# Windowed attention ahead of a mixture of experts: score and value products over 128 and 64 rows with zeros beside, and a transposition that moves to TensorE

## The chip, the cores and the metric

The kernel runs on one core of a Trainium2 chip. The metric is the device time of one execution in microseconds (us). A core has five engines with a queue of instructions each: TensorE (PE in the rows; its weight loads are PEld), VectorE (DVE), ScalarE (ACT), GpSimd (POOL) and SyncE (SP), which here only starts DMAs. Engines wait for each other through semaphores.

## The reference

```python
# q, k, v: (8 batches, 8 heads, 576 tokens, 64); window = 32; dilation = 4
rel = pos[:, None] - pos[None, :]
mask_plain = (rel >= 0) & (rel < window)                                   # heads 0 to 3
mask_dil = (rel >= 0) & (rel < window * dilation) & (rel % dilation == 0)   # heads 4 to 7
attn = softmax(where(mask, q @ k.T / sqrt(64), -1e9));  out = attn @ v
x = out.transpose(0, 2, 1, 3).reshape(4608, 512)
logits = x @ w_gate                       # (4608, 8)
expert_idx = argmax(logits); gate_w = softmax(logits)[expert_idx]
for e in range(8):                        # at most 80 tokens, those of largest gate_w
    out[tok] = gate_w[tok] * (relu(x[tok] @ w1[e]) @ w2[e])   # other rows stay zero
```

Everything is float32. Each w1[e] is 512 x 1024, each w2[e] 1024 x 512.

## The kernel before

**Attention.** For the dilated heads the host orders the tokens by their residue modulo 4, so that both kinds of head look at 32 keys back. A block of 32 queries then needs 64 keys: its own block and the one before. Work goes in 36 tiles (t). A tile holds four blocks j of 32 queries of the plain heads (hh = 0) and four of the dilated heads (hh = 1), 32 x 4 = 128 partitions by 8 x 64 scores. `plan` says which blocks; a batch is 4.5 tiles.

The steps of a tile, with engine and line:

- `scores` on TensorE: the additive mask goes into PSUM by four products with an identity (L393), then 32 products of 64 rows of q and k, 32 weight columns and 64 keys each (L400). A float32 product stands in the trace as two matmuls, so 32 read as x64.
- `smax`, `sbias` on DVE: maximum over each 64 keys (L407) and its scaled negative (L411).
- `sexp` on ACT: eight exponentials of 128 x 64, each with its own bias (L417).
- `ptrans` on DVE: a transposition in 32 x 32 squares (L421) gives the probabilities with keys on partitions.
- `pv` on TensorE: 16 products of 32 keys, with block-diagonal values `v4` of four heads side by side, 260 columns (64 values and a one for the sum, times four) (L435).
- `raw` on ACT (L443) copies that out of PSUM, `norm_r` on DVE (L447, L448) takes the reciprocal of the sums, `norm` on POOL (L454) multiplies, in two halves; the last tile's two halves are on DVE. x is stored (xs).
- `xtrans` on TensorE (four 128 x 128 transpositions, L460) and `xcopy` on ACT (L485) give x with features on partitions, for the gate.

**Routing.** Per batch: gate products (L532, L538), a softmax and the chosen expert on DVE (L560 to L592), counts (`KLp` L643; `csp` L686, of the last batch `tail`; `pre` L692), then a merge with the best 80 tokens of the earlier batches (TensorE `msa`, `msb`, `msr`, `msl`; one-hot rows `ol`, `or`; the new list `lstf`, L808). A batch's merge needs the one before it. After merge 7 `irow` (L1033) holds the rows to gather.

**Experts.** Weights arrive as 512 KB chunks `wr`, and each is split into a high part `wh` (ACT, L189) and a low part `wl` (DVE or POOL, L191); expert 0's chunks are split in halves of 128 x 512. Rows are gathered (`xg`, L285), transposed (`tx`, L1055) and multiplied three times per chunk (`hp` L1072, `yps` L1104). The 18 `zero_out` DMAs of 512 KB clear the output.

**Order.** Each engine's queue is fixed when the kernel is built: `drive` takes chains of work (tiles, gates, counts, merges, splits), and each time appends the piece with the smallest sum of its estimated start and a penalty from a table of numbers. DMAs from SP go in the order of the code; `load_q`, `load_k`, `load_v` and `load_mask` are called around the scores.

## Time and profile before

| | |
|---|---|
| median of three runs | 346.96 us (342.06 to 353.88) |
| profiled execution, its own time | 343.53 us |
| its span in the profile | 341.8 us |
| mean granted TensorE clock (of full speed) | 0.969 |
| busy: PE, PEld, DVE, ACT, POOL | 89%, 61%, 66%, 62%, 55% of the span |
| attention from the third tile's scores to the last value product | about 17 to 196 us |
| from there to `irow` | about 196 to 231 us |
| experts | about 231 to 342 us |

The own time is 1.73 us above the span: that lies outside the recorded instructions. Rows of the profile are in us from the start of the span, unless ns is said.

### The profile page before, as it was taken

What the parts mean: (1) busy time and instruction counts of PE and PEld (TensorE: products, weight loads), DVE (VectorE), ACT (ScalarE), POOL (GpSimd) and SP (SyncE); (2) the same over time, 40 slices, a digit from 0 to 9 for tenths busy, and PEclk for the clock granted to TensorE, in tenths of its full rate; (3) what the DMA queues carried; (4) which work ended last, traced back from release to release, by engine and by line L of the source; (5) the groups of instructions that cost most, each with busy time, mean ns of one, the idle gap of its engine ahead of it and who ended that gap; (6) DMA issues with size and microseconds to landing.
All of it is one profiled execution on the core that took longest, in us unless ns stands there. A gap on an engine that the chain in (4) does not pass through costs nothing.

```text
span 341.8 us, 12863 instructions
## 1 busy us (share of the span) xinstructions
PE 304.0 (89%) x5255; PEld 207.6 (61%) x5255; DVE 224.4 (66%) x628; ACT 213.3 (62%) x620; POOL 186.6 (55%) x281
## 2 busy tenths in 40 slices
PE   6398899989699897899899988776999999999993
PEld 6364666756566664666567557665566666656561
DVE  4233264858366585487576988731589999999950
ACT  6437486667485656667659960110798798789560
POOL 9012134462752385338629789004597889755613
PEclk9789899999999999999999999986899999999999
DMA  6989988979979999999987594701546999999101
GB/s 187 247 241 315 282 269 282 293 223 315 279 222 288 320 360 382 347 278 343 348 288 273 174 311 188 238 10 40 155 149 180 372 397 365 393 344 357 43 0 38
DMA packets 38731, 86.62 MB, mean 253 GB/s; under 512 B 4368, under 2 KB 15504, under 8 KB 38672
## 3 DMA queue, kind: packets, MB, share of 16 engines
q1 hardware_dynamic: 37392, 83.17, 74.4%
q0 software_dynamic: 1280, 2.62, 2.4%
q8 instruction: 41, 0.67, 0.8%
q14 instruction: 18, 0.15, 0.1%
HBM read 65.59 MB, written 20.19 MB: 251 GB/s over the span
## 4 chain that ended last, share of the span: by engine, by line
PE 68%; issue 10%; DMA 8%; DVE 8%; ACT 3%; POOL 1%; SPq 1%; POOLq 0%; ACTq 0%; DVEq 0%
PE pv L435 20%; PE sc L400 9%; PE hp L1072 9%; PE yps L1104 8%; PE xt L460 6%; DVE wl L191 4%; PE sc L393 3%; DMA mask<-in_mask 2%; PE warm L328 2%; PE lt L532 2%; PE KLp L643 2%; DMA out<-yo,itok 2%; DMA wr<-in_w 2%; DMA k<-in_k 1%; DMA xg<-xs,irow 1%
## 5 line engine op out<-in xcount | busy, mean ns | idle before, releaser
L191 DVE TENSOR_TENSOR wl<-wr,wh 128x1024 fp32r<-128x1024 f32 (+1 forms) x53 | 84.1, 1640 | 6.7 <-ACT wh L189 5.9
L454 POOL TENSOR_TENSOR x<-xr,rc 128x256 f32<-128x256 f32 x70 | 42.5, 629 | 84.1 <-ACT xr L443 44.8
L435 PE MATMUL pv<-v,pts 128*32 128x260 f32 x1152 | 75.8, 393 | 5.6 <-issue 5.1
L417 ACT ACTIVATE ex<-sc,nb 128x64 f32<-128x64 f32 x288 | 65.0, 340 | 22.0 <-DVE nb L411 21.9
L189 ACT CAST wh<-wr 128x1024 fp32r<-128x1024 f32 (+1 forms) x72 | 65.8, 959 | 8.4 <-DMA wr<-in_w 4.1
L435 PEld LDWEIGHTS pv<-v,pts 128*32 128x32 f32 x1152 | 36.9, 110 | 29.3 <-issue 7.9
L191 POOL TENSOR_TENSOR wl<-wr,wh 128x1024 fp32r<-128x1024 f32 (+1 forms) x19 | 43.9, 2315 | 9.3 <-ACT wh L189 9.1
L400 PE MATMUL sc<-k,q 64*32 64x64 f32 x2304 | 40.3, 220 | 1.3 <-issue 1.2
L400 PEld LDWEIGHTS sc<-k,q 64*32 64x32 f32 x2304 | 38.3, 109 | 4.8 <-issue 1.5
L443 ACT COPY xr<-pv 128x520 f32<-128x520 f32 x35 | 21.2, 607 | 28.3 <-PE pv L435 25.6
L407 DVE TENSOR_REDUCE mx<-sc 128x8 f32<-128x512 f32 x36 | 24.4, 678 | 21.6 <-PE sc L400 21.5
L285 POOL DMA_INDIRECT xg<-xs,irow x16 | 23.9, 1493 | 24.7 <-DVE lstf L1035 16.8
L485 ACT COPY xT<-xt 128x256 f32<-128x256 f32 (+5 forms) x114 | 32.9, 400 | 6.3 <-PE xt L460 6.1
L421 DVE STREAM_TRANSPOSE pts<-ex 128x512 f32<-128x512 f32 x36 | 25.3, 704 | 9.7 <-ACT ex L417 8.7
L328 PE MATMUL warm<-ones 128*128 128x128 bf16 x317 | 26.0, 237 | 2.4 <-DVE ones L320 1.0
L460 PE MATMUL xt<-c_ident,x 128*128 128x128 f32 x144 | 24.3, 286 | 4.3 <-issue 3.5
L1072 PE MATMUL hp<-wh,xh 128*80 128x512 f32 x64 | 26.9, 420 | 0.4 <-ACT xh L1062 0.4
L447 DVE TENSOR_SCALAR rc<-xr 128x8 f32<-128x8 f32 x35 | 6.1, 175 | 32.1 <-ACT xr L443 31.9
L1104 PE MATMUL yps<-wh,hlo 128*80 128x512 f32 x64 | 25.4, 397 | 1.1 <-DVE hlo L1092 1.1
L1072 PE MATMUL hp<-wl,xh 128*80 128x512 f32 x64 | 26.1, 409 | 0.0
L1072 PE MATMUL hp<-wh,xl 128*80 128x512 f32 x64 | 26.1, 408 | 0.0
L460 PEld LDWEIGHTS xt<-c_ident,x 128*128 128x128 f32 x144 | 15.2, 140 | 16.8 <-issue 11.7
(133 smaller groups left out, 491.1 us busy)
## 6 DMA issues: line engine op xcount, KB each, us to landing
wr<-in_w SPq DMA_DIRECT2D x64, 512.0 KB, 8.0
v<-in_v SPq DMA_DIRECT2D x72, 130.0 KB, 5.7
...
```

Of the source, the lines that this page charges most:

```text
L189: nc.scalar.copy(hi[:, s], w[:, s])
L191: eng.tensor_tensor(out=lo[:, s], in0=w[:, s], in1=hi[:, s].bitcast(F32), op=ALU.subtract)
L328: nc.tensor.matmul(out=t[:, 0:P], lhsT=ones, rhs=ones, start=True, stop=True, skip_group_check=True)
L400: nc.tensor.matmul(out=ps[32 * c:32 * c + 32, 4 * hh + j, :], lhsT=q[64 * u:64 * u + 64, hh, g, j, :], rhs=k2[b % 2][64 * u:64 * u + 64, 2 ...
L417: nc.scalar.activation(st[t]["ex"][:, m], st[t]["sc"][:, m], AF.Exp, bias=st[t]["nb"][:, m:m + 1], scale=1.0 / float(D) ** 0.5)
L421: nc.vector.transpose(out=pt.rearrange("p a b c d -> p (a b c d)"), in_=st[t].pop("ex").rearrange("p a c -> p (a c)"))
L435: nc.tensor.matmul(out=ps[32 * j:32 * j + 32, hh, 0:HS].rearrange("p (c d) -> p c d", c=4), lhsT=pt[:, hh, j, half, :], rhs=v4[vt // 2 % N ...
L454: eng.tensor_tensor(out=x[:, h], in0=st[t][of][:, h, :, :, 0:D], in1=st[t]["rc"][:, h].unsqueeze(3).broadcast_to([P, 2, 2, D]), op=ALU.mult)
L460: nc.tensor.transpose(out=st[t]["xt"][:, c, :], in_=x[:, c * P:(c + 1) * P], identity=ident)
L485: copy(out=dst, in_=ps[:, HC * hh:HC * hh + HC, col:col + n])
L1072: nc.tensor.matmul(out=fs[e]["hp"][n][0:C], lhsT=a_[:, c, :], rhs=b_[:, sl], start=(c == 0 and q == 0), stop=(c == NKC - 1 and q == 2))
L1104: nc.tensor.matmul(out=fs[e]["y"][0:C], lhsT=a_[:, f, :], rhs=b_[:, sl], start=(f == 0 and q == 0), stop=(f == NFC - 1 and q == 2))
```

## The change

- Scores: q and k now have feature and head of a pair interleaved on the partitions (2d + u). `k2` has a second column plane: on the rows of head u the keys stand in plane u, and the other plane is zero. One product of 128 rows, 32 weight columns and 128 columns gives both heads: 16 products per tile for 32.
- The mask is held once for each different pattern, 128 x 2 x 64, and read by a repeating view; it is loaded in two DMAs.
- Softmax: DVE subtracts the maximum from PSUM into SBUF (`ssub`, L415), and one exponential of 128 x 512 works in place on ACT (L420).
- The probabilities are transposed by four 128 x 128 transpositions on TensorE into a PSUM tile `pT` (L426), and copied out in three pieces, two on ACT (64 partitions x 256, L432) and one on DVE (64 partitions x 512, L434), into two fixed buffers `pts` whose other places stay zero.
- Values: 24 products per tile of 64 keys of two heads, 130 columns (L454), for 16 of 32 keys and 260 columns. `v4` has zeros beside the values in the same way.
- `norm` is one operation per tile for two. The gate and the counts share one PSUM buffer (`lt`), and the gate of a batch waits for the counts of the one before.
- Keys of a batch come in two DMAs, those of batch 0 in three pieces of two. More buffers are cleared at the start (DVE, POOL, ACT).
- Ten `zero_out` DMAs go beside the tiles, one every third tile; eight follow the last tile.
- The table of numbers of `drive` is another, and so is the order of the last batch's blocks.

```diff
-ZR, ZI, IW, W0, W1, W2, XC, SP0 = 2, 18, 8, 40, 15, 30, 1, 2
+ZR, ZI, IW, W0, W1, W2, XC, SP0 = 2, 6, 8, 40, 15, 30, 1, 2
-l_pe, lat, LA, AGE = -0.011, 0.147, 3, 0.165
+l_pe, lat, LA, AGE = -0.011, 0.147, 5, 0.162
...
-        k2 = [qp.tile([P, NG, KW], F32, name=f"k2_{i}") for i in range(2)]
+        k2 = [qp.tile([P, 2, KW + HB], F32, name=f"k2_{i}") for i in range(2)]
-        v4 = [vp.tile([P, 4, 2, 4, 2, D + 1], F32, name=f"v4_{i}") for i in range(NV)]
+        v4 = [vp.tile([P, 2, 4, 2, 2, D + 1], F32, name=f"v4_{i}") for i in range(NV)]
+        pts = [kp.tile([P, 2, 2, 2, 2, 2, 32], F32, name=f"pts_{i}") for i in range(2)]
...
+        KS = (0, 64, 160, HB)
+        kv = [k[:, :, 0:KW].rearrange("p u (a x) -> p u a x", a=2 * NG) for k in k2]
         nc.vector.memset(zero, 0.0)
-        nc.vector.memset(k2[0][:, :, 0:32], 0.0)
+        for u in range(2):
+            nc.vector.memset(kv[0][:, u, :, 0:KS[1]], 0.0)
+        for i in (1, 2):
+            for u in range(2):
+                (nc.vector, nc.gpsimd)[u].memset(kv[0][:, u, :, KS[i]:KS[i + 1]], 0.0)
...
+        for i in range(2):
+            for u in range(2):
+                nc.scalar.copy(v4[i][:, u].rearrange("p c a g d -> p (c a g) d"), z65)
+        for i in range(2):
+            nc.vector.memset(pts[i], 0.0)
+        for u in range(2):
+            nc.gpsimd.memset(k2[1][:, u, 0:KW], 0.0)
+        for u in range(2):
+            nc.gpsimd.memset(v4[2][:, u], 0.0)
+        def load_k(b, lo=0, hi=HB):
+            for u in range(2):
...
-        def load_k(b, lo=0, hi=S):
-            nc.sync.dma_start(k2[b % 2][:, :, 32 + lo:32 + hi], io["k"][b, :, :, lo:hi])
+                    nc.sync.dma_start(kv[b % 2][u::2, u, :, lo:hi], io["k"][b, u].rearrange("d (a x) -> d a x", a=2 * NG)[:, :, lo:hi])
...
         def scores(t):
 
             q = q2[t // 2 % NQ][:, t % 2]
-            ps = ps2.tile([P, 8, 64], F32, tag="sc", name=f"sc_{t}")
-            for c in range(4):
-                rows = slice(64 * (c // 2), 64 * (c // 2) + 64)
-                nc.tensor.matmul(out=ps[32 * c:32 * c + 32].rearrange("p a k -> p (a k)"), lhsT=identb[rows, 32 * c:32 * c + 32],
-                                 rhs=mask[rows, t % TPP].rearrange("p a k -> p (a k)"), start=True, stop=False, skip_group_check=True)
-            for hh in range(2):
+            ps = ps2.tile([P, NG, 2, 2, 32], F32, tag="sc", name=f"sc_{t}")
+            for j in range(4):
+                nc.tensor.matmul(out=ps[32 * j:32 * j + 32].rearrange("p (h g) u a k -> p h (g u) (a k)", h=2), lhsT=identb[:, 32 * j:32 * j + 32],
+                                 rhs=mask[:, sig[t]].unsqueeze(2).broadcast_to([P, 2, 4, 64]), start=True, stop=False, skip_group_check=True)
+            for a in range(NG):
                 for j in range(4):
-                    b, k = qplan[t][hh][j]
-                    for c in range(4):
-                        u, g = c // 2, c % 2
-                        nc.tensor.matmul(out=ps[32 * c:32 * c + 32, 4 * hh + j, :], lhsT=q[64 * u:64 * u + 64, hh, g, j, :],
-                                         rhs=k2[b % 2][64 * u:64 * u + 64, 2 * hh + g, 32 * k:32 * k + 64],
-                                         start=False, stop=True, skip_group_check=True)
+                    b, k = qplan[t][a // 2][j]
+                    o, w = a * S + 32 * (k // 2), HB if k % 2 or k == 0 else HB - 32
+                    nc.tensor.matmul(out=ps[32 * j:32 * j + 32, a], lhsT=q[:, a // 2, a % 2, j, :],
+                                     rhs=k2[b % 2][:, :, o:o + 2 * w].rearrange("p u (r y) -> p u r y", r=2)[:, :, :, 0:32],
+                                     start=False, stop=True, skip_group_check=True)
             st[t] = {"sc": ps}
...
-            nc.vector.tensor_reduce(out=st[t]["mx"], in_=st[t]["sc"], axis=AX.X, op=ALU.max)
-
-        def sbias(t):
-            st[t]["nb"] = sp.tile([P, 8], F32, tag="nb", name=f"nb_{t}")
-            nc.vector.tensor_scalar(out=st[t]["nb"], in0=st[t]["mx"], scalar1=-1.0 / float(D) ** 0.5, scalar2=None, op0=ALU.mult)
-
-        def sexp(t, hh):
-            if hh == 0:
-                st[t]["ex"] = sp.tile([P, 8, 64], F32, tag="ex", name=f"ex_{t}")
-            for m in range(4 * hh, 4 * hh + 4):
-                nc.scalar.activation(st[t]["ex"][:, m], st[t]["sc"][:, m], AF.Exp, bias=st[t]["nb"][:, m:m + 1], scale=1.0 / float(D) ** 0.5)
+            nc.vector.tensor_reduce(out=st[t]["mx"], in_=st[t]["sc"].rearrange("p a u r k -> p (a u) (r k)"), axis=AX.X, op=ALU.max)
+        def ssub(t):
+            st[t]["ex"] = sp.tile([P, NG, 64, 2], F32, tag="ex", name=f"ex_{t}")
+            nc.vector.tensor_tensor(out=st[t]["ex"].rearrange("p a k u -> p a u k"), in0=st[t].pop("sc").rearrange("p a u r k -> p a u (r k)"),
+                                    in1=st[t].pop("mx").rearrange("p (a u) -> p a u", u=2).unsqueeze(3).broadcast_to([P, NG, 2, 64]), op=ALU.subtract)
+        def sexp(t):
+            e = st[t]["ex"].rearrange("p a k u -> p (a k u)")
+            nc.scalar.activation(e, e, AF.Exp, scale=1.0 / float(D) ** 0.5)
 
         def ptrans(t):
-            pt = sp.tile([P, 2, 4, 2, 32], F32, tag="pts", name=f"pts_{t}")
-            nc.vector.transpose(out=pt.rearrange("p a b c d -> p (a b c d)"), in_=st[t].pop("ex").rearrange("p a c -> p (a c)"))
-            st[t]["pt"] = pt
+            st[t]["pT"] = ps1.tile([P, NG, 2, 2, 32], F32, tag="pT", name=f"pT_{t}")
+            ex = st[t].pop("ex")
+            for a in range(NG):
+                nc.tensor.transpose(out=st[t]["pT"][:, a].rearrange("p i e q -> p (i e q)"), in_=ex[:, a].rearrange("p k u -> p (k u)"), identity=ident)
+        def pcopy(t, half):
+            ps = st[t]["pT"].rearrange("p (h g) i e q -> p h g e i q", h=2)
+            if half == 0:
+                for h in range(2):
+                    nc.scalar.copy(pts[t % 2][0:64, h, :, :, h], ps[0:64, h])
+            else:
+                nc.vector.tensor_copy(out=pts[t % 2][64:P].rearrange("p h g e s i q -> p (h g) (e s) i q")[:, :, 1:3],
+                                      in_=ps[64:P].rearrange("p h g e i q -> p (h g) e i q"))
 
         def pv(t):
 
-            pt = st[t]["pt"]
             ps = ps1.tile([P, 2, 512], F32, tag="pv", name=f"pv_{t}")
-            for hh in range(2):
-                for half in range(2):
-                    for j in range(4):
-                        b, k = qplan[t][hh][j]
-                        prev = (b, k - 1) if 32 * k % (S if hh == 0 else S // DIL) else (b, k)
-                        vt, vi = vpos[hh, (b, k) if half else prev]
-                        assert vt // 2 * 2 - 1 <= t and (t <= vt // 2 * 2 + 2 or vt // 2 + NV >= NT // 2)
-                        nc.tensor.matmul(out=ps[32 * j:32 * j + 32, hh, 0:HS].rearrange("p (c d) -> p c d", c=4), lhsT=pt[:, hh, j, half, :],
-                                         rhs=v4[vt // 2 % NV][:, :, vt % 2, vi, hh, :],
-                                         start=(half == 0), stop=(half == 1), skip_group_check=True)
-            st[t]["pv"] = ps[:, :, 0:HS].rearrange("p a (u g d) -> p a u g d", u=2, g=2)
+            work = [[] for _ in range(4)]
+            for j in range(4):
+                for h in ((0, 1), (1, 0))[j % 2]:
+                    b, k = qplan[t][h][j]
+                    assert k % 2 == (j + h) % 2
+                    cols = [(0, k)] + [(1, k - 1)] * (k % 2 == 0 and 32 * k % (S if h == 0 else S // DIL) > 0)
+                    for g in range(2):
+                        for i, (s, kk) in enumerate(cols):
+                            vt, vi = vpos[h, (b, kk)]
+                            assert vt // 2 * 2 - 1 <= t and (t <= vt // 2 * 2 + 2 or vt // 2 + NV >= NT // 2), (t, vt)
+                            work[j].append((h, g, s, vt // 2 % NV, vt % 2 * 2 + vi, i == 0, i == len(cols) - 1))
+            for n in range(max(len(w) for w in work)):
+                for j in range(4):
+                    for h, g, s, vb, vc, first, last in work[j][n:n + 1]:
+                        nc.tensor.matmul(out=ps[32 * j:32 * j + 32, h, 2 * g * (D + 1):2 * (g + 1) * (D + 1)].rearrange("p (u d) -> p u d", u=2),
+                                         lhsT=pts[t % 2][:, h, g, j % 2, s if h == 0 else 1 - s, j // 2, :], rhs=v4[vb][:, :, vc, h, g, :],
+                                         start=first, stop=last, skip_group_check=True)
+            st[t]["pv"] = ps[:, :, 0:HS].rearrange("p h (a d) -> p h a d", a=4)
...
-            x = st[t]["x"].rearrange("p (a g u) d -> p a u g d", a=2, g=2)
-            for h in range(2):
-                eng.tensor_tensor(out=x[:, h], in0=st[t][of][:, h, :, :, 0:D], in1=st[t]["rc"][:, h].unsqueeze(3).broadcast_to([P, 2, 2, D]), op=ALU.mult)
+            eng.tensor_tensor(out=st[t]["x"].rearrange("p (h a) d -> p h a d", h=2), in0=st[t][of][:, :, :, 0:D],
+                              in1=st[t]["rc"].unsqueeze(3).broadcast_to([P, 2, 4, D]), op=ALU.mult)
...
+            while b and not end and ("pre", b - 1) not in ev:
+                yield None
...
-                kps = ps1.tile([P, 512], F32, tag="ct", name=f"KLp_{b}_{i}")
+                kps = ps1.tile([P, 512], F32, tag="lt", name=f"KLp_{b}_{i}")
...
         load_q(0, slice(0, 1))
-        load_k(0, 0, P)
+        load_k(0, 0, KS[1])
         nc.sync.dma_start(identb, io["identb"])
-        load_mask(0)
+        NM = mask.shape[1]
+        load_mask(0, 2)
         load_q(0, slice(1, 2))
-        load_k(0, P, 2 * P)
-        load_mask(1)
+        load_k(0, KS[1], KS[2])
+        nc.sync.dma_start(ident, io["ident"])
+        load_v(0)
         load_q(1)
-        load_k(0, 2 * P, 3 * P)
-        load_v(0)
-        load_mask(2)
-        load_k(0, 3 * P, S)
-        nc.sync.dma_start(ident, io["ident"])
+        load_mask(2, NM)
+        load_k(0, KS[2], KS[3])
         load_v(1)
-        load_mask(3)
...
+            if ZI <= i < NT and i % 3 == 0:
                 zero_out(zeros.pop(0))
+            if i == NT + 1:
+                while zeros:
+                    zero_out(zeros.pop(0))
```

On TensorE, before, around tile 24 (the numbers behind a name are tile and buffer):

```order
L435 MATMUL pv_21_2712<-v4_1_147,pts_21_2621 32x260 x16
L460 MATMUL xt_20_2743<-c_ident_66,x_20_2688 128x128 x4
L393 LDWEIGHTS c_identb_96
L393 MATMUL sc_24_2756<-mask_95,c_identb_96 32x512
...
L400 MATMUL sc_24_2756<-k2_1_143,q2_0_144 32x64 x32
```

The same place after, where a transposition of probabilities (`pT`) comes into the row:

```order
L426 MATMUL pT_22_2489<-c_ident_66,ex_22_2313 128x128 x4
L396 LDWEIGHTS c_identb_96
L396 MATMUL sc_24_2504<-c_mask_95,c_identb_96 32x512
...
L403 MATMUL sc_24_2504<-k2_1_143,q2_0_144 32x128 x16
L454 MATMUL pv_21_2534<-v4_1_147,pts_1_150 32x130 x24
L478 MATMUL xt_20_2565<-c_ident_66,x_20_2527 128x128 x4
```

sc_24 stood between pv_21 and pv_22; now it stands ahead of pv_21, behind the transposition of tile 22.

On DVE, before, behind the last tile, from the counts of batch 7 on:

```order
L689 TENSOR_REDUCE pre_7_4522<-W_7_4520 128x5
L692 TENSOR_TENSOR pre_7_4522<-pre_7_4522,tail_4428 128x5
L191 TENSOR_TENSOR wl_0_4_4434<-wr_0_4_1794,wh_0_4_4433 128x512 x2
L191 TENSOR_TENSOR wl_0_5_4457<-wr_0_5_2053,wh_0_5_4456 128x512 x2
L191 TENSOR_TENSOR wl_0_6_4535<-wr_0_6_2263,wh_0_6_4534 128x512 x2
L191 TENSOR_TENSOR wl_0_7_4564<-wr_0_7_2524,wh_0_7_4563 128x512
L808 COPY lstf_68<-msl_5_4767 80x72
L771 TENSOR_SCALAR th_6_4787,r0_6_4788<-msb0_6_4821,gate_w_153 128x80 x5
L784 TENSOR_SCALAR rr_6_4853<-msr_6_4847,c_pack_97 80x8
L720 SCALAR_TENSOR_TENSOR r0_6_4788<-pre_6_4063,r0_6_4788 128x5
L708 TENSOR_TENSOR ol_6_4856<-c_pack_97,r0_6_4788 128x400
L708 TENSOR_TENSOR or_6_4858<-c_pack_97,rr_6_4853 80x640
```

The same place after:

```order
L712 TENSOR_TENSOR pre_7_4173<-pre_7_4173,tail_4036 128x5
L740 SCALAR_TENSOR_TENSOR r0_7_4228<-pre_7_4173,r0_7_4228 128x5
L728 TENSOR_TENSOR ol_7_4336<-c_pack_97,r0_7_4228 128x400
L1048 TENSOR_REDUCE irow_71<-tail_4036 80x16
L1050 COPY lstf_68<-tail_4036 80x72
L1052 SCALAR_TENSOR_TENSOR tt_72<-lstf_68 80x8
L1053 TENSOR_SCALAR un_73<-lstf_68 80x8
L1054 TENSOR_TENSOR itok_70<-un_73,tt_72 80x8
L1055 TENSOR_TENSOR gsel_69<-lstf_68 80x8
L1056 TENSOR_TENSOR gsel_69<-lstf_68,gsel_69 80x8
L193 TENSOR_TENSOR wl_0_0_4333<-wr_0_0_713,wh_0_0_4332 128x512
L193 TENSOR_TENSOR wl_0_1_4428<-wr_0_1_911,wh_0_1_4427 128x512 x2
```

Between the counts of batch 7 and `irow` there stood seven halves of `wl_0`, the list of merge 5 and the whole of merges 6 and 7; now only the end of merge 7 is left there, and the halves of `wl_0` all stand behind `irow`.

## Rows read from the trace of the kernel before

**Rows 1.** The page's chain of the work that ended last, by engine.

```profile
PE 68%; issue 10%; DMA 8%; DVE 8%; ACT 3%; POOL 1%; SPq 1%; POOLq 0%; ACTq 0%; DVEq 0%
```

**Rows 2.** Busy time in stretches of the span: start and end, length; busy us (instructions) of PE, PEld, DVE, ACT, POOL; granted TensorE clock, busy share of the DMA engines, GB/s.

```profile
0.00:17.00 17.00, 8.82 (x204) 8.03 (x208) 6.16 (x18) 8.74 (x21) 8.43 (x17) 0.89 0.85 217
17.00:30.00 13.00, 12.39 (x306) 7.63 (x296) 5.05 (x13) 6.53 (x25) 2.37 (x4) 0.88 0.94 253
30.00:50.00 20.00, 17.49 (x456) 12.87 (x459) 8.35 (x27) 12.75 (x54) 4.75 (x8) 0.91 0.93 284
50.00:75.00 25.00, 23.71 (x623) 15.74 (x619) 15.72 (x62) 17.05 (x64) 13.60 (x33) 1.00 0.87 273
197.00:231.00 34.00, 27.88 (x365) 21.50 (x365) 23.70 (x102) 8.32 (x29) 16.44 (x33) 0.96 0.53 186
231.00:300.00 69.00, 66.15 (x338) 43.58 (x336) 55.33 (x50) 51.62 (x72) 53.22 (x29) 0.95 0.74 260
17.00:197.00 180.00, 165.68 (x4193) 111.88 (x4183) 109.74 (x437) 119.71 (x466) 89.24 (x194) 0.98 0.91 291
```

**Rows 3.** TensorE's timeline over one tile and a gate: start, length (us), line, tile, shape, count. Lengths overlap; from one start to the next is what a group costs.

```profile
60.66 1.96 PE L435 MATMUL pv<-v,pts 128*32 128x260 f32 x32
62.55 0.66 PE L460 MATMUL xt<-c_ident,x 128*128 128x128 f32 x4
63.13 0.40 PE L393 MATMUL sc<-mask,c_identb 64*32 64x512 bf16 x4
63.36 1.06 PE L400 MATMUL sc<-k,q 64*32 64x64 f32 x64
64.35 1.08 PE L532 MATMUL lt<-xT,wg 128*32 128x128 f32 x32
65.25 0.30 PE L538 MATMUL lt<-xT,wg 128*32 128x64 f32 x8
65.48 0.66 PE L460 MATMUL xt<-c_ident,x 128*128 128x128 f32 x4
65.97 0.47 PE L686 MATMUL csp<-ones,gtl 128*128 128x1 bf16 x13
```

**Rows 4.** Groups of instructions in 17 to 197 us: busy us and mean ns of one, then the engine's idle time ahead of them and what ended it.

```profile
L417 ACT ACTIVATE ex<-sc,nb 128x64 f32<-128x64 f32 x272 | 61.5, 341 | 18.3 <-DVE nb L411 18.2
L454 POOL TENSOR_TENSOR x<-xr,rc 128x256 f32<-128x256 f32 x70 | 42.5, 629 | 84.1 <-ACT xr L443 44.8 <-DVE rc L448 26.4 <-DMA v<-in_v 6.4
L421 DVE STREAM_TRANSPOSE pts<-ex 128x512 f32<-128x512 f32 x35 | 24.7, 705 | 9.7 <-ACT ex L417 8.7 <-PE pv L435 1.0
L407 DVE TENSOR_REDUCE mx<-sc 128x8 f32<-128x512 f32 x34 | 23.0, 677 | 16.7 <-PE sc L400 16.6
L411 DVE TENSOR_SCALAR nb<-mx 128x8 f32<-128x8 f32 x34 | 7.1, 208 | 0.4
```

**Rows 5.** What TensorE waited for in 17 to 197 us: total us, times, longest. "issue" is a wait for nothing that the profile shows.

```profile
PE pv L435 <- issue: 5.1, 4, 2.4
PE xt L460 <- issue: 3.5, 2, 2.5
PE lt L532 <- issue: 2.8, 2, 2.4
```

**Rows 6.** TensorE's timeline at the start, with the idle time ahead in brackets.

```profile
5.86 0.62 PE L393 MATMUL sc<-mask,c_identb 64*32 64x512 bf16 x4 [0.36 <-DMA mask<-in_mask]
...
16.39 0.61 PE L393 MATMUL sc<-mask,c_identb 64*32 64x512 bf16 x4 [5.08 <-DMA mask<-in_mask]
```

**Rows 7.** DVE's timeline at the start.

```profile
1.05 0.48 DVE L342 MEMSET zero<- 128x512 f32 x1
```

**Rows 8.** TensorE's timeline at the last value product.

```profile
193.86 1.97 PE L435 MATMUL pv<-v,pts 128*32 128x260 f32 x32
195.76 0.53 PE L686 MATMUL csp<-ones,gtl 128*128 128x1 bf16 x15
196.15 0.43 PE L766 MATMUL msb<-KRT,ohT 128*128 128x320 bf16 x2
```

**Rows 9.** DVE's timeline behind it, to `irow`.

```profile
195.44 1.71 DVE L191 TENSOR_TENSOR wl<-wr,wh 128x512 fp32r<-128x512 f32 x2
...
197.65 0.76 DVE L454 TENSOR_TENSOR x<-pv,rc 128x256 f32<-128x256 f32 x2
...
205.51 0.68 DVE L191 TENSOR_TENSOR wl<-wr,wh 128x512 fp32r<-128x512 f32 x1
...
209.91 0.16 DVE L692 TENSOR_TENSOR pre<-pre,tail 128x5 f32<-128x5 f32 x1 [0.79 <-PE tail L686]
210.08 6.64 DVE L191 TENSOR_TENSOR wl<-wr,wh 128x512 fp32r<-128x512 f32 x7
...
222.83 0.23 DVE L808 COPY lstf<-msl 80x72 f32<-80x72 f32 x1 [0.63 <-PE msl L802]
...
230.70 0.19 DVE L1033 TENSOR_REDUCE irow<-tail 80x16 int32<-80x32 f32 x1 [1.56 <-PE tail L802]
```

**Rows 10.** TensorE's timeline where the experts begin.

```profile
235.09 0.53 PE L1055 MATMUL tx<-c_ident,xg 80*128 80x80 f32 x2 [2.20 <-DMA xg<-xs,irow]
...
236.00 0.72 PE L1072 MATMUL hp<-wh,xh 128*80 128x512 f32 x1 [0.38 <-ACT xh L1062]
...
238.65 0.47 PE L1055 MATMUL tx<-c_ident,xg 80*128 80x80 f32 x2
```

More of the change, by code (lines that the diff above doesn't have):

```diff
@@ L58, in plan @@
                 lst[t0 + k][1] = seq[4 * k:4 * k + 4]
+    for t in q:
+        t[1] = [t[1][i] for i in (1, 0, 3, 2)]
     return q, v
@@ L304, in moe_attn_kernel @@
         NQ = 2
-        mask = kp.tile([P, TPP, 8, 64], BF16, name="mask")
+        mask = const("mask", BF16, kp)
         identb = const("identb", BF16, kp)
```

132 lines of the change are left out of this document (53 added, 79 removed).

## Prediction

> **What bounds the kernel now.** I read the chain of waits first: TensorE carries 68% of it, "issue" 10%, DMA and DVE 8% each [rows 1]. Then the stretches [rows 2]: from 17 to 197 us TensorE is busy 165.68 of 180.00 us, DVE 109.74, ACT 119.71, POOL 89.24. So the attention is bound by TensorE, which idles only 14.3 us there, and 11.4 of these are "issue" waits, eight of them, of up to 2.5 us [rows 5], in a stretch whose DMA share is 0.91. From 197 to 231 us, the merges between the last value product and the gathers, TensorE is still busy, but what ends last is a chain of small steps, and DVE's queue holds other work between them [rows 9]. The experts from 231 us are TensorE again, 66.15 of 69.00 us. An edit therefore pays on TensorE's row of work per tile, on the issue waits, or in the tail; work taken from ACT and POOL does not move the end by itself.
>
> **The change part by part,** against the profiled execution's own 343.5 us.
>
> *Start, +3.* The first keys' DMA has to wait for DVE to clear that piece too; the nearest row is a memset of 512 elements at 0.48 us [rows 7], two of them, so +1.0. The third tile's scores wait today 5.08 us for a DMA [rows 6], so bytes in the queue decide. Counted from the shapes, 3.28 MB are issued up to the piece that tile 2 needs, for 2.67 MB up to its mask before: 0.61 MB at the 217 GB/s of that stretch [rows 2] is 2.8 us. Some of the 1.0 lies beside that. Bounds 0 (order of landing kinder than order of issue) to +6; I take +3.
>
> The Trainium skill ("DMA: Bandwidth & Descriptors", Specifications) says that a descriptor under 512 B falls short of line rate and is read, modified and written. The first two pieces of the keys have 256 B and 384 B, 0.79 MB together; at half rate that would be some 3.4 us more, an estimate from that page with the 217 to 235 GB/s of this queue, and no run here shows it. By it the start would be +6, the upper bound above.
>
> *TensorE's work per tile, +0.03 us each, +1 in all.* Before, from start to start [rows 3]: value products 1.89, transposition of x 0.58, mask 0.23, scores 0.99; 3.69 in all. After: the mask's four products keep 512 columns, 0.23. The 16 score products have the shape of the gate's row (128 rows, 32 weight columns, 128 columns, x32): 64.35 to 65.25 is 0.90; the bound above is today's 0.99. The 24 value products read as x48 of 130 columns: by the gate's row 0.90 x 48/32 x 130/128 = 1.37; by today's value products per column 1.89 x (48 x 130)/(32 x 260) = 1.42. The new transposition is the form of L460: 0.49 (65.48 to 65.97) to 0.58. x again 0.58. Sum 3.57 to 3.80; I take the upper half, 3.72, because smaller products leave more places to wait. Over 36 tiles +1 (-4 to +4).
>
> *What moves into the attention, +2.* The planner's new order has the list of merge 5 and most of merge 6 done ahead of the last value product (as the two orders of DVE show). One such step on TensorE, msb, takes 0.43 [rows 8]; five of them (msl of merge 5, and msa, msb, msr, and the transpositions around them, of merge 6) are 2.2. This work was in the tail and is counted out there.
>
> *Issue waits, -4.* They come to 11.4 us [rows 5]. Eight clears of 512 KB (4.2 MB) leave this stretch, the masks shrink from 1.79 to 0.43 MB (from their shapes), keys come in fewer and longer pieces, and TensorE has 12 matmuls less per tile in the trace's count (92 for 104). 180 us at 291 GB/s are 52.4 MB; without 5.5 MB that is a tenth less. Bounds: 0, and -9 if nearly all of it goes. I take a third, since the profile names no cause.
>
> *DVE, +2.5.* Per tile go a transposition of 0.705 and a scaling of 0.208 [rows 4]; there come a subtraction of 512 elements from PSUM, which I price at the maximum's 0.677 for the same read, and a copy of 64 x 512 out of PSUM, the same. Over the 36 tiles 36 x 1.354 - 31.8 = +17 on 109.7 of 180 us, before the one-hots that move in. That is 70% busy. The steps of a tile now lie in one row: scores, maximum, subtraction, exponential, pT on TensorE, copies, value products, two engine changes more than before. What hides it is the longer lead: sc_24 stands ahead of pv_21 instead of ahead of pv_22, so a tile's scores have 3.7 us more. If that cover is gone the wait is paid per tile: bounds 0 and +8 (0.22 per tile); I take +2.5.
>
> *ACT and POOL, 0.* Eight exponentials of 341 ns [rows 4] are 2.7 us per tile; one of 512 elements I price at the copy-like 0.6. With two copies of 256 ACT gains about a microsecond per tile. It has 60 us idle already, mostly behind DVE. One multiply for two on POOL likewise: idle 84.1 us. TensorE hides both; they would count only if DVE's row above became late.
>
> *Tail, -15.5.* Before, from the end of the last value product (195.76, [rows 8]) to `irow` (230.70, [rows 9]) it is 34.9 us. Three things go. First, from 210.07, where the counts of batch 7 are done, to 222.83, where merge 6 hands over its list, are 12.8 us: 6.64 of low parts for expert 0, then the end of merge 5 and merge 6. In the new order merge 6 has only its last step open there, and no low part stands in the way. Second, two low parts of 1.71 us stand ahead of the last tile's normalisation [rows 9], of which 1.35 are waited. Third, one half of 0.68 and the tile's shorter value products, some 1.5 with what then runs side by side. Sum 15.6. Walking DVE's new queue step by step with the old lengths I come to 19.1 us from the last value product to `irow`, that is -15.8. Bounds -13 and -18; I take -15.5. Late next are the gates and counts of batch 7, then merge 7's own chain.
>
> *Experts, +1.* The twelve halves that DVE now splits behind `irow` are 12 x 0.68 = 8.2 us [rows 9]. But the first product starts 5.3 us behind `irow` anyway (230.70 to 236.00), and two chunks of halves feed it for 2.65 us (236.00 to 238.65, [rows 10]), against 1.36 us of DVE for one chunk: DVE keeps ahead unless it starts late. The eight late clears meet a DMA share of 0.53 [rows 2]. Bounds 0 and, if all halves were late, +8; I take +1, the cover being DMA and DVE time free at 231 us.
>
> Sum: 3 + 1 + 2.2 - 4 + 2.5 - 15.5 + 1 = -9.8, so 343.5 becomes 333.7. The median of the runs is 3.4 above the profiled execution and the lowest run 1.5 below, so an own time of 333.7 stands for a median of about 334 to 337: **336 us**.
>
> **The rivals.**
>
> *A larger gain.* The issue waits go nearly whole (-9 for -4) and the start costs nothing (0 for +3): 343.5 - 9.8 - 5 - 3 = 325.7, about 327 as a median. For it: the waits lie in the stretch with 0.91 DMA share, which the change relieves. Against: 0.91 less a tenth is still much.
>
> *The gain is given back: no change.* Either DVE becomes the bound, with 0.35 us per tile waited (36 x 0.35 = 12.6), or the splits that left the tail return as waits of the experts (+8) beside a tail that saves less. 333.7 + 10 to 12 = 344 to 346. For it: 17 us more on DVE, and every half of expert 0 moved behind `irow`. Against: DVE idles 70 us now, and TensorE needs a chunk only every 1.3 us.
>
> *The clock falls: slower.* Each tile would have eight transpositions for four and half the score products, and the gated clock could stay low. The granted clock was 0.88 and 0.91 in 17 to 50 us, after a wait of 5.08 us [rows 2, 6], and 1.00 in 50 to 75. At 0.88 all through the attention its 165.68 us would be 165.68 x (0.98/0.88 - 1) = 18.8 longer: 352.5, as a median some 356. It uses up the gain below a mean clock of 0.925, and is slower by 2% below about 0.89. Against: 1.00 with four transpositions in every tile.
>
> The Trainium skill ("TensorE: Matmul & The Clock Gate", Part 4, PE-mode transpose) says that transpositions do not count as work for the clock gate. By that rule this rival has its mechanism; the trace so far does not bear it out, with 1.00 granted while x was transposed in every tile.
>
> **How the numbers follow.** The forecast has 0.55 (own range 330 to 343), the larger gain 0.13, no change 0.20, the clock 0.12. The range takes in the larger gain's upper half and no change, and leaves out what is under 325 and the clock's case: 325 to 350. A measurement of this kernel tells about 2% from no change: faster is under 340.0, slower above 353.9. Of the forecast's 0.55 some 0.08 lie above 340: faster 0.47 + 0.13 = 0.60, slower 0.12, the rest 0.28.
>
> **What would show it.** Right: the third tile's scores near 19 us; about 3.7 us of TensorE per tile; `irow` some 19 us behind the last value product, at about 216; issue waits of 5 to 9 us; the clock at 0.97 or more behind 50 us. Wrong: waits of pT, or of the value products, for DVE or ACT in most tiles (the cover of three tiles is too short); the first `hp` products waiting for `wl`; a clock near 0.9 in 50 to 197 us; a start of the third tile behind 23 us.

## Result, and the profile after

The changed kernel takes 327.72 us (median of 4 runs, 326.13 to 331.89); beside it the kernel before took 344.51 (339.79 to 353.88). The ratio is 0.9597, 95% interval 0.9492 to 0.9702: faster by 4.0%. The profiled execution took 326.13 us (span 324.3), where that of before took 343.53. Executions of one kernel differ by some us with the clock granted in the tail (the stretch from the last value product to `irow`), so a tail is compared below only with its clock beside it.

The span in three stretches, cut at the end of the last value product and at `irow` (columns as in [rows 2]), before:

```profile
0.00:195.83 195.83, 173.40 (x4370) 119.23 (x4371) 114.74 (x454) 127.28 (x485) 96.50 (x210) 0.97 0.91 285
195.83:230.70 34.87, 28.68 (x381) 21.88 (x382) 24.57 (x101) 9.49 (x32) 17.61 (x34) 0.97 0.54 189
230.70:341.80 111.10, 101.95 (x510) 66.45 (x508) 85.11 (x74) 76.50 (x105) 72.49 (x38) 0.96 0.62 218
```

and after:

```profile
0.00:194.08 194.08, 175.42 (x3904) 144.28 (x3904) 138.79 (x468) 108.59 (x382) 82.43 (x151) 0.98 0.74 257
194.08:213.41 19.33, 14.92 (x205) 11.02 (x206) 15.28 (x84) 8.38 (x26) 5.91 (x17) 1.00 0.96 342
213.41:324.30 110.89, 101.22 (x510) 65.73 (x507) 81.57 (x86) 79.75 (x113) 74.84 (x41) 0.95 0.71 258
```

The tail gave 15.5 us, the attention (all before it) 1.8, the experts 0.2. DVE's timeline in the tail after, at the list of merge 6, the counts of batch 7 and `irow`:

```profile
204.71 0.23 DVE L828 COPY lstf<-msl 80x72 f32<-80x72 f32 x1
...
211.68 0.16 DVE L712 TENSOR_TENSOR pre<-pre,tail 128x5 f32<-128x5 f32 x1
...
213.41 0.18 DVE L1048 TENSOR_REDUCE irow<-tail 80x16 int32<-80x32 f32 x1 [0.75 <-PE tail L822]
```

From the last value product to the end of these counts it is 17.8 us, where it was 14.2 before; from there to `irow` 1.6, where it was 20.6 [rows 9]. Merge 6 and most of merge 7 now lie ahead of the counts.

Up to the last value product TensorE is busy 2.0 us longer and idle 3.8 us less. Its longest waits in 17 to 196 us (total, times, longest) answer to [rows 5]:

```profile
PE pv L454 <- issue: 4.1, 5, 1.9
PE sc L403 <- issue: 2.7, 3, 1.8
PE sc L403 <- DMA k<-in_k: 2.5, 1, 2.5
PE msl L818 <- DVE ol L728: 1.0, 2, 0.7
PE pT L426 <- DVE mx L410: 0.8, 1, 0.8
```

Issue waits are 6.8 us, where it was 12.8 before (both up to the last value product). Waits for DVE are small, though DVE is busier by 24 us. One tile on TensorE, in the manner of [rows 3]:

```profile
26.19 0.63 PE L426 MATMUL pT<-c_ident,ex 128*128 128x128 f32 x4
26.74 0.40 PE L396 MATMUL sc<-c_mask,c_identb 128*32 128x512 bf16 x4
26.97 1.04 PE L403 MATMUL sc<-k,q 128*32 128x128 f32 x32
27.84 1.51 PE L454 MATMUL pv<-v,pts 128*32 128x130 f32 x48
29.28 0.66 PE L478 MATMUL xt<-c_ident,x 128*128 128x128 f32 x4
29.78 0.60 PE L426 MATMUL pT<-c_ident,ex 128*128 128x128 f32 x4
```

From start to start these cost 0.55 (transposition of probabilities), 0.23 (mask), 0.87 (scores), 1.44 (value products) and 0.50 (transposition of x); 3.59 us in all, for 3.69 before.

### The profile page after: what moved, and what is told of

Read it like the earlier page. It is cut to its first block, busy times and chain, and to the rows that moved or that the text cites. A ratio compares the mean times of both kernels' runs of the same rounds, so it can differ in the third digit from the quotient of the medians.

```text
span 324.3 us, 11403 instructions
## 1 busy us (share of the span) xinstructions
PE 291.6 (90%) x4615; PEld 221.0 (68%) x4615; DVE 235.6 (73%) x636; ACT 196.7 (61%) x519; POOL 163.2 (50%) x208
## 4 chain that ended last, share of the span: by engine, by line
PE 50%; DMA 15%; DVE 14%; issue 8%; ACT 7%; POOL 3%; SPq 1%; POOLq 0%; ACTq 0%; DVEq 0%
PE pv L454 10%; PE sc L403 8%; PE hp L1087 7%; PE yps L1119 7%; PE xt L478 4%; PE pT L426 4%; DMA wr<-in_w 4%; DMA out<-zero 3%; DVE wl L193 3%; DMA k<-in_k 3%; PE sc L396 3%; DMA xs<-x 2%; DVE pts L434 2%; ACT wh L191 2%; ACT xT L503 2%
## 5 line engine op out<-in xcount | busy, mean ns | idle before, releaser
L471 POOL TENSOR_TENSOR x<-xr,rc 128x512 f32<-128x512 f32 x35 | 36.9, 1055 | 78.2 <-DVE rc L467 33.8
L454 PE MATMUL pv<-v,pts 128*32 128x130 f32 x1664 | 56.6, 274 | 4.1 <-issue 4.1
L454 PEld LDWEIGHTS pv<-v,pts 128*32 128x32 f32 x1664 | 47.0, 108 | 7.7 <-issue 7.0
L403 PE MATMUL sc<-k,q 128*32 128x128 f32 x1152 | 42.8, 289 | 6.2 <-DMA k<-in_k 3.5
L193 POOL TENSOR_TENSOR wl<-wr,wh 128x1024 fp32r<-128x1024 f32 (+1 forms) x18 | 41.0, 2282 | 14.4 <-PE yps L1119 7.5
L403 PEld LDWEIGHTS sc<-k,q 128*32 128x32 f32 x1152 | 35.5, 116 | 11.3 <-issue 8.1
L503 ACT COPY xT<-xt 128x64 f32<-128x64 f32 (+3 forms) x195 | 33.6, 312 | 13.1 <-PE xt L478 12.8
L434 DVE COPY pts<-pT 64x512 f32<-64x512 f32 x36 | 25.0, 694 | 19.3 <-ACT pts L432 18.8
L432 ACT COPY pts<-pT 64x256 f32<-64x256 f32 x72 | 23.7, 381 | 12.3 <-PE pT L426 12.2
L420 ACT ACTIVATE ex<-ex 128x512 f32<-128x512 f32 x36 | 23.0, 638 | 12.1 <-DVE ex L415 11.7
L415 DVE TENSOR_TENSOR ex<-sc,mx 128x512 f32<-128x512 f32 x36 | 24.8, 689 | 4.7 <-PE pT L426 3.8
L1119 PE MATMUL yps<-wh,hh 128*80 128x512 f32 x64 | 25.3, 395 | 0.0
L1119 PE MATMUL yps<-wl,hh 128*80 128x512 f32 x64 | 25.0, 391 | 0.0
```

Source lines behind the costliest of these rows:

```text
L193: eng.tensor_tensor(out=lo[:, s], in0=w[:, s], in1=hi[:, s].bitcast(F32), op=ALU.subtract)
L403: nc.tensor.matmul(out=ps[32 * j:32 * j + 32, a], lhsT=q[:, a // 2, a % 2, j, :], rhs=k2[b % 2][:, :, o:o + 2 * w].rearrange("p u (r y) -> ...
L415: nc.vector.tensor_tensor(out=st[t]["ex"].rearrange("p a k u -> p a u k"), in0=st[t].pop("sc").rearrange("p a u r k -> p a u (r k)"), in1= ...
L432: nc.scalar.copy(pts[t % 2][0:64, h, :, :, h], ps[0:64, h])
L434: nc.vector.tensor_copy(out=pts[t % 2][64:P].rearrange("p h g e s i q -> p (h g) (e s) i q")[:, :, 1:3], in_=ps[64:P].rearrange("p h g e i ...
L454: nc.tensor.matmul(out=ps[32 * j:32 * j + 32, h, 2 * g * (D + 1):2 * (g + 1) * (D + 1)].rearrange("p (u d) -> p u d", u=2), lhsT=pts[t % 2 ...
```

## Experiments

In a row of stretches the last three numbers are the granted clock, the busy share of the DMA engines and GB/s, as in [rows 2].

**The order without the data flow.**

The batches from which the one-hots go to another engine, the look-ahead, and the penalties (three more lines, left out here):

```diff
-FB, CB, TE, NWA, XC0 = 6, 5, 35, 8, 2
+FB, CB, TE, NWA, XC0 = 3, 6, 34, 8, 2
...
-l_pe, lat, LA, AGE = -0.011, 0.147, 3, 0.165
+l_pe, lat, LA, AGE = -0.011, 0.147, 5, 0.162
...
```

> The kernel before with the planner's numbers of the changed one (look-ahead, penalties, which engine makes the one-hots) and nothing else: its own data flow, its own zero_out DMAs beside the tiles. Theory 'order': the 15 us of the tail come from the order alone. From the end of the last value product to irow it takes 19 to 22 us (34.9 before, 19.4 in the changed kernel), the experts stay at 111 us, the attention grows by 2 to 4 us for the merge work that moves in: 329 to 332 us, ratio 0.95 to 0.97. Rival 'data flow': the tail only gets short because the changed attention leaves DVE and ACT room; with the old attention the moved merges and one-hots push the attention out by 8 us or more, the tail stays above 25 us, and the time is within 2% of the kernel before.

Measured: 339.85 us, ratio to the kernel before 0.9898 (0.9847 to 0.9948). Attention and tail, then TensorE's longest waits for DVE in 17 to 200 us:

```profile
0.00:205.81 205.81, 177.78 (x4397) 121.27 (x4397) 114.14 (x468) 124.68 (x480) 87.52 (x186) 0.95 0.84 270
205.81:226.20 20.39, 15.79 (x227) 12.12 (x227) 15.55 (x82) 9.40 (x29) 7.64 (x18) 1.00 0.49 157
```

```profile
PE msr L779 <- DVE th L771: 3.7, 3, 1.4
PE msa L751 <- DVE oh L578: 3.4, 2, 1.8
PE KLp L643 <- DVE key L586: 2.5, 1, 2.5
```

Both theories are half right. The tail is 20.4 us with the order alone, but the attention grows by 10.0: TensorE is busy 4.4 us longer, at a clock of 0.95 for 0.97, and idle 5.6 longer. Merge and count steps, which stand in TensorE's queue ahead of the tiles, wait 10.6 us for DVE, where it was 0.6 before. The issue waits fall at the same time, from 12.8 us to 6.3. Two thirds of what the tail gained are given back.

**The data flow without the order.** The same lines the other way round, in the changed kernel.

> The changed kernel with the numbers of the kernel before in the planner (p_pt, which had no value there, kept). Its order then leaves msb and msr of merge 6 behind the last value product, and puts several halves of wl_0 ahead of irow again. Theory 'order': from the last value product to irow 25 to 31 us for 19.4, the time 332 to 337 us, 2% to 3% over the changed kernel. Rival 'data flow': 21 us or less and 326 to 329 us.

Measured: 344.08 us, ratio to the kernel before 0.9979 (0.9934 to 1.0024): none of the gain is left, worse than either theory. Attention and tail, and TensorE's longest wait:

```profile
0.00:199.70 199.70, 173.38 (x3898) 143.89 (x3898) 140.31 (x456) 113.31 (x391) 99.99 (x189) 0.96 0.72 250
199.70:229.48 29.78, 24.94 (x227) 19.05 (x228) 20.41 (x98) 8.23 (x26) 14.80 (x24) 0.60 0.94 348
```

```profile
PE pT L426 <- DVE pts L434: 10.9, 9, 1.6
```

```profile
94.07 0.60 PE L426 MATMUL pT<-c_ident,ex 128*128 128x128 f32 x4
...
96.54 0.63 PE L426 MATMUL pT<-c_ident,ex 128*128 128x128 f32 x4 [1.64 <-DVE pts L434]
```

The tail grows as expected, but with the granted clock at 0.60 in it, so what the order alone does there is not separated from the clock. The attention grows by 5.6 us: in this order pT of one tile stands six times with no step of a tile between it and pT of the tile before (the two rows are pT_15 and pT_16), and waits until DVE has copied that out of the one PSUM buffer, up to 1.6 us. In the changed kernel's order there is no such pair. The issue waits are only 1.8 us here.

**The clears.** In the kernel before, ten beside the tiles and eight behind; in the changed kernel, all beside the tiles:

```diff
-ZR, ZI, IW, W0, W1, W2, XC, SP0 = 2, 18, 8, 40, 15, 30, 1, 2
+ZR, ZI, IW, W0, W1, W2, XC, SP0 = 2, 6, 8, 40, 15, 30, 1, 2
...
-            if ZI <= i < NT and zeros:
+            if ZI <= i < NT and i % 3 == 0:
                 zero_out(zeros.pop(0))
+            if i == NT + 1:
+                while zeros:
+                    zero_out(zeros.pop(0))
...
-        for z in zeros:
-            zero_out(z)
```

This is the kernel before; in the changed kernel the line of `ZI` and the first condition go the other way.

> The kernel before with the zero_out DMAs as in the changed one (ten beside the tiles, one every third, eight behind the last tile), nothing else. Theory 'bytes': the issue waits of TensorE follow the DMA traffic beside them; 4.2 MB less take them from 12.6 to 7 to 9 us in 17 to 196 us, the attention gets 3 to 6 us shorter. Rival 'instructions': they follow the number of TensorE instructions, which is the same: 11 to 14 us, the attention as before within 1 us. In both the tail is the same within 1 us (its DMA share was 0.53); the time 338 to 341 by 'bytes', 342 to 345 by the rival.

> The changed kernel with all zero_out DMAs beside the tiles, one per tile from tile 18 on, as before. Theory 'bytes': issue waits rise from 6.7 to 10 to 13 us, the time is 3 to 6 us longer (329 to 332). Rival 'instructions': issue waits 5 to 8 us and the time within 1.5 us of the changed kernel.

Measured: 345.76 us, ratio to the kernel before 0.9977 (0.9926 to 1.0028), and 328.41, ratio 0.9529 (0.9501 to 0.9558). Issue waits were 14.4 us (12.8 before) and 8.6 (6.8 in the changed kernel): moving 4.2 MB in or out of the stretch did not lower or raise them by the amounts of 'bytes'. (The attention of the first run is 3.7 us longer than before in its profiled execution, 199.5 for 195.8, against the 1 us that 'instructions' allowed; its median shows nothing of it.) The waits stand at places of the program. Here is the fifth value product, of the changed kernel and of this one with all clears beside the tiles:

```profile
38.53 1.28 PE L454 MATMUL pv<-v,pts 128*32 128x130 f32 x36
40.85 0.42 PE L454 MATMUL pv<-v,pts 128*32 128x130 f32 x4 [1.04 <-issue]
```

```profile
36.86 1.28 PE L454 MATMUL pv<-v,pts 128*32 128x130 f32 x36
38.65 0.42 PE L454 MATMUL pv<-v,pts 128*32 128x130 f32 x4 [0.51 <-issue]
```

Both stop behind the same one of the value product's matmuls, the 36th as the trace counts, and only the length differs. The page counts 41 packets of the instruction queue before and 36 after, for 5255 and 4615 matmuls. The moved bytes don't fit these waits, but the length of the program alone doesn't either: with the order alone they are 6.3 us at 5127 matmuls and 40 packets, with the data flow alone 1.8 at 4631 and 36. So they change with TensorE's order. In those two runs TensorE waited longer for DVE; whether that is the reason was not tested, and that the issue waits are instruction loading is not shown. The tail of the second run shows something else, its clock:

```profile
193.65:216.97 23.32, 19.54 (x204) 15.28 (x205) 15.44 (x84) 10.02 (x28) 5.91 (x17) 0.68 0.36 114
```

TensorE's tail has the same instructions as in the changed kernel, at 0.68 for 1.00, and takes 4.0 us longer.

**The low parts out of the tail of before.**

```diff
-e_split, e_splitd, p_split, p_splitd, p_splitp, q_hi, q_lo, q_lop = 0.457, 0.713, -0.188, -0.69, 1.436, 1.204, 1.134, -1.508
+e_split, e_splitd, p_split, p_splitd, p_splitp, q_hi, q_lo, q_lop = 0.457, 40.0, -0.188, 40.0, 40.0, 1.204, 1.134, -1.508
```

> The kernel before, but every low part of expert 0's weights stands behind irow (penalties of 40 for them in the planner); TensorE's order and the merges stay as they were. It measures one half of the tail's term by itself. Theory 'both count': the low parts held 6.6 us of the chain ahead of the list of merge 5 and some 2 us more, so from the end of the last value product to irow it takes 26 to 28 us for 34.9, the experts stay within 1 us of 111, the time is 2% shorter (337 to 340). Rival 'the merges alone': the chain of merges is late anyway and the tail stays above 32 us. Rival 'paid back': the tail shrinks, but the first experts wait for their low parts and the stretch behind irow grows by 5 us or more.

Measured: 345.60 us (345.06 to 346.65), inside the range of the kernel before beside it (339.71 to 351.19), ratio 1.0152 (1.0069 to 1.0235): no gain. The tail is 35.57 us, at a clock of 0.87 for 0.97. DVE, then TensorE, where the low parts had been:

```profile
212.70 0.16 DVE L692 TENSOR_TENSOR pre<-pre,tail 128x5 f32<-128x5 f32 x1 [2.84 <-PE tail L686]
218.38 0.23 DVE L808 COPY lstf<-msl 80x72 f32<-80x72 f32 x1 [5.53 <-PE msl L802]
...
232.56 0.19 DVE L1033 TENSOR_REDUCE irow<-tail 80x16 int32<-80x32 f32 x1 [1.69 <-PE tail L802]
```

```profile
207.00 5.28 PE L328 MATMUL warm<-ones 128*128 128x128 bf16 x40
212.08 0.58 PE L686 MATMUL tail<-ones,gtl 128*128 128x1 bf16 x15
212.52 5.36 PE L328 MATMUL warm<-ones 128*128 128x128 bf16 x64
217.72 0.35 PE L798 MATMUL msl<-vals,ol 128*80 128x72 bf16 x5
```

DVE now waits 5.53 us for the list of merge 5, and TensorE reaches it behind 64 warming products. The 6.64 us of low parts in [rows 9] had lain beside these. The lower clock costs about 2 us ahead of the counts (the first 40 warming products took 5.28 us, where it was 3.26 before), so the tail as a whole is no fair measure. From the end of the counts to `irow`, where the 64 took 5.36 for 5.25, it is 19.7 us for 20.6: of the 6.64 us only 0.9 was on the path.

**Half of the warming products as well.**

```diff
-                    warm(NWA, ps1, "xt", [512])
+                    warm(NWA // 2, ps1, "xt", [512])
```

> The kernel before with the low parts of expert 0 behind irow, and half of the warming products that the planner puts into TensorE's queue behind the last tiles (4 for each 8; nothing that the result needs). In the run without the low parts the tail stayed at 35.6 us, and 104 warming products stood in TensorE's queue ahead of the list of merge 5. Theory 'TensorE's queue': these products, not the low parts, held the merges: with half of them the tail goes from 35.6 to 26 to 30 us, unless the granted clock falls in it, which is read from its rows. Rival 'the chain of merges': 33 us or more at an equal clock.

Measured: 346.73 us, tail 34.03:

```profile
196.72:230.75 34.03, 28.50 (x265) 20.53 (x266) 16.07 (x90) 9.37 (x32) 9.26 (x28) 0.62 0.22 70
```

```profile
210.12 5.07 PE L328 MATMUL warm<-ones 128*128 128x128 bf16 x32
```

Inconclusive: the clock fell towards the lower of its two levels (a granted 0.50 is 1.2 of 2.4 GHz) for most of the tail, and 32 products took as long (158 ns each) as 64 had (84 ns). Over the whole execution the mean clock was 0.931 to 0.943 in the four runs, and 0.963 to 0.973 in the four with all warming products.

**Transpositions, subtraction and exponential, each made larger in the changed kernel.**

```diff
-            for a in range(NG):
+            for a in list(range(NG)) * 2:
                 nc.tensor.transpose(out=st[t]["pT"][:, a]...
```

> The changed kernel with every transposition of probabilities on TensorE made twice (eight per tile instead of four, same result). Theory 'TensorE's row': 36 x 0.58 = 21 us more, the clock at 1.00 in 50 to 190 us as now: 345 to 349 us. Rival 'clock': with twelve transpositions in every tile the granted clock of 50 to 190 us falls under 0.95 and the time passes 355 us. Rival 'hidden': TensorE has slack per tile, under 10 us more.

> The changed kernel with DVE's subtraction made twice in every tile (same result): 36 x 0.69 = 25 us more on DVE, which is busy 127 of 173 us beside the tiles. Theory 'covered': TensorE's row ends last and the scores lead far enough, so at most a third of it shows: 327 to 336 us. Rival 'DVE at the edge': TensorE waits for DVE in most tiles and 15 us or more come through, 342 us and above.

> The changed kernel with the exponential of a tile made in eight pieces of 64 columns instead of one of 512 (same result): at 341 ns each against 0.64 us in one, 36 x 2.09 = 75 us more on ACT, which is busy 109 of the 194 us up to the last value product. Theory 'ACT has room': 184 of 194 us still fit, but in a row of steps with two copies behind, so that about a tenth shows: 5 to 12 us more. Rival 'hidden altogether', as the prediction priced ACT at nothing: under 3 us. Rival 'ACT is the bound': 15 us or more, TensorE waits for ex or pts in nearly every tile.

Measured: 336.40, 337.35 and 330.72 us; ratios to the kernel before 0.9855 (0.9726 to 0.9984), 0.9874 (0.9727 to 1.0021) and 0.9565 (0.9475 to 0.9655). The attention of each, in this order:

```profile
0.00:204.77 204.77, 185.90 (x4048) 157.47 (x4048) 138.79 (x468) 111.58 (x382) 82.24 (x151) 0.98 0.71 244
```

```profile
0.00:203.38 203.38, 173.79 (x3904) 143.89 (x3904) 162.51 (x504) 108.51 (x382) 82.66 (x151) 0.97 0.71 245
```

```profile
0.00:197.55 197.55, 173.10 (x3904) 142.04 (x3904) 138.89 (x468) 129.06 (x634) 82.45 (x151) 0.98 0.73 252
```

With four more transpositions the attention is 10.7 us longer, by TensorE's busy time (10.5). A group of eight stands in TensorE's row like this:

```profile
101.40 1.07 PE L426 MATMUL pT<-c_ident,ex 128*128 128x128 f32 x8
102.40 0.40 PE L396 MATMUL sc<-c_mask,c_identb 128*32 128x512 bf16 x4
```

From start to start eight cost 1.00 us here and 0.97 in the median tile, and four cost 0.54 in the changed kernel: 0.42 to 0.43 us per tile for the 0.58 expected, some 15 us over 36 tiles. Nothing of it is hidden. The busy time grows by less because other work was cheaper in this execution: added up from start to start, scores 2.6 us, value products and warming products 1.0 each, in part for a better clock at the start (0.81 in 17 to 30 us for 0.74). The median is only 8.7 us longer, under the 10 of 'hidden', but not for the reason that this rival gives. The clock rival falls; with twelve transpositions in every tile the row of 50 to 190 us reads

```profile
50.00:190.00 140.00, 130.97 (x2911) 110.71 (x2914) 101.94 (x378) 78.13 (x282) 60.30 (x118) 1.00 0.74 257
```

With the subtraction made twice DVE is busy 24 us longer, of which 9.3 come through (39%), a little over the third of 'covered'; the median is 9.6 longer, just above that theory's range. Eight exponentials cost ACT 20.5 us of busy time (255 ns each, and they overlap), for the 75 expected, of which 3.5 come through: between the two theories, but at about a quarter of the cost that both reckoned with.

**The look-ahead, and the first keys' pieces.** `LA` 3 for 5; `KS = (0, 64, 192, HB)` for `(0, 64, 160, HB)`; and both.

> The changed kernel with a look-ahead of 3 tiles in the planner for 5, all other numbers as in it. The scores then stand one value product later (sc_24 behind pv_21). Theory 'cover': the longer lead hides the two engine changes of the new softmax; without it TensorE waits for DVE and ACT (pT for pts, value products for pts) by 0.15 to 0.4 us per tile, 5 to 14 us, 332 to 342 us. Rival: the lead is worth nothing, 326 to 330 us.

> The changed kernel with the pieces of the first keys cut at 192 instead of 160 columns of 288, so that the third tile's scores need two pieces and not three, and the second piece has 512 B per row for 384 B. Theory 'bytes ahead': the second tile's scores come 0.5 us later, the third's no longer wait 2.5 us for keys, and TensorE doesn't fall to the low clock there (1.92 us for a tile's scores between 18.8 and 24 us against 1.04 later): the first value product at 20 to 22 us for 24.6, and the time 2 to 4 us shorter. Rival: the mask, the identity or the values are next, first value product at 23.5 us or later.

> Both the look-ahead of 3 and the cut of the first keys at 192 columns: 2 to 4 us under the run with the look-ahead of 3 alone, so 321 to 324 us at the median, if the start's theory holds; no better than 325 otherwise.

Measured: 325.37 us (319.79 to 331.67), 328.27 (322.13 to 331.21), 321.92 (318.89 to 325.15). With the shorter look-ahead the attention is 191.17 us, not longer but 2.9 shorter than in the changed kernel: TensorE waits 2.4 us longer for DVE, and 3.1 less in issue waits. So the lead of scores over value products was little of a cover. With the other pieces the third tile's scores no longer stop for keys, though their wait for the mask is longer (3.93 us for 1.62), and the first value product comes at 21.29 us for 24.57. The changed kernel, and that one:

```profile
18.79 1.92 PE L403 MATMUL sc<-k,q 128*32 128x128 f32 x28 [2.54 <-DMA k<-in_k]
```

```profile
16.36 1.95 PE L403 MATMUL sc<-k,q 128*32 128x128 f32 x32
...
21.29 1.54 PE L454 MATMUL pv<-v,pts 128*32 128x130 f32 x40
```

Alone it does not show in the median (328.27 for 327.72): its attention ends at 194.21 again, with two issue waits of over 2 us. With both, all four runs lie below the fastest of the changed kernel:

```profile
0.00:186.81 186.81, 171.23 (x3901) 142.97 (x3902) 137.87 (x471) 106.68 (x382) 82.08 (x151) 0.98 0.78 267
186.81:206.10 19.29, 15.77 (x218) 11.75 (x219) 15.32 (x81) 9.46 (x28) 8.02 (x19) 1.00 0.92 322
```

It is 1.8% under the changed kernel by medians, the kernel before having taken 346.25 us beside it. By medians it is also under each half, but its runs and those of the shorter look-ahead overlap.

## Why the prediction was right, and where it was not

The direction, the size within the range and the stretch were right; the median came 8.3 us below the forecast, and the attention and not the tail made the difference. Against the profiled executions (-9.8 forecast, -17.4 measured), term by term:

| term | forecast | measured |
|---|---|---|
| start: TensorE's waits for DMA | +3 | 7.1 to 6.4: -0.7 |
| work per tile and merges moved in | +3.2 | busy 173.4 to 175.4: +2.0 |
| issue waits | -4 | 12.8 to 6.8: -6.0 |
| waits for DVE and the rest | +2.5 | 2.4 to 4.7: +2.3 |
| tail | -15.5 | 34.87 to 19.33: -15.5 |
| experts | +1 | 111.10 to 110.89: -0.2 |

The first four come to -2.4 by the waits and the busy time, and -1.8 by the stretch's end.

- **Start.** About right in size, but not by the wait that the sum named. The third tile's scores end later (20.65 us for 18.64), by 2.0 and not 3, while the waits for DMA are 0.7 shorter. What is longer is the scores themselves: the first four tiles' took 1.92 to 1.95 us (before only the third's, 1.94), where 1.04 is usual later, at a granted clock of 0.74 in 17 to 30 us for 0.88 before. The table has this under busy time. It depends on the execution: in the run with all clears beside the tiles, which has the same order on TensorE, the first two tiles' scores took 1.08, and TensorE is busy 171.8 us up to the last value product, not 175.4. That the bytes ahead decide fits the run with two pieces for three, where the wait of 2.54 us was gone. The pieces of 256 and 384 B are 0.66 MB (two of 128 KB, two of 192 KB) and not 0.79, which makes the prediction's estimate of 3.4 us for them about 2.9. That keys of 256 and 384 B per row land slower, as the Trainium skill has it ("DMA: Bandwidth & Descriptors", Specifications), no run here separates from the bytes.
- **TensorE's tile.** 3.59 us, the low end of 3.57 to 3.80: the scores' 0.87 were priced from the gate's row at 0.90, the value products' 1.44 from the gate's row at 1.37 and from the old ones at 1.42. The upper half was taken for a reason that the trace did not bear out. The merge products that moved in come to 2.3 us more (10.5 for 8.2, added up from start to start), as forecast (2.2).
- **Issue waits.** Right in sign, low in size (the prediction's 11.4 are three lines; two smaller ones make it 12.8), and for the wrong cause: the clears' bytes have no effect that shows, in either kernel. The new order alone brings them to 6.3 us, the new data flow alone to 1.8. What sets them stays open.
- **DVE.** Right: 24 us more on it, little waited. But the cover named for it, the longer lead, is worth only some 2.4 us of these waits by the run with a look-ahead of 3. What the order must avoid is another thing, two transpositions in a row on one PSUM buffer.
- **Tail.** The sum was right to the tenth and its parts were wrong. The step that took 6.64 us of low parts off the path fails: without them only 0.9 us of these is gained. What went is TensorE's own row, the end of merge 5 and merge 6, with the warming products that the planner put between them (232 up to `irow` before, 88 after, added up from TensorE's timeline). The interval from 210.07 to 222.83 left as a whole, so the total hid the error. The other two parts (1.35 and 1.5 us ahead of the counts) did not come: that stretch grew by 3.5. Instead 6.3 us of merge 7's chain, which the sum left in place (222.83 to 230.70 before, 1.6 us after), now lie beside the counts. -12.8 + 3.5 - 6.3 is again -15.6, and that is luck; the walk along DVE's new queue, with 19.1 us for the 19.33 measured, was the better support. And the 15.5 holds at a clock of 1.00: the run with the clears beside the tiles has the same tail at 0.68 and 23.3 us, and the changed kernel's other executions, 1 to 6 us longer, had mean clocks of 0.956 to 0.962 for 0.974.
- **Experts.** Right within its bounds: the first products waited 0.2 us in all for `wl`.
- **What the sum lacked.** It put the tail's gain to the order without a condition. Order alone gives 1.0%, the data flow alone nothing that can be told, both 4.0%. The rival 'given back', at 0.20, is what each of the halves does: the order by waits of merges for DVE, the data flow by pT's buffer and a low clock (means of 0.931 to 0.957 in its eleven runs, for 0.956 to 0.974 in the changed kernel's). Why the same order has so much less of the merge waits beside the new data flow is not settled.
- **The clock.** Refuted: 1.00 in 50 to 190 us with eight and with twelve transpositions per tile. The rule of the Trainium skill ("TensorE: Matmul & The Clock Gate", Part 4, PE-mode transpose) would have let the clock fall there; beside this much other TensorE work no row shows it. The clock does fall in the tail of other runs (0.60 with the data flow alone) and behind the waits at the start (0.74 in 17 to 30 us).
